# Fused attention, convolution gate and spectral mixing on one core: three moves of small work in the first stage

## The chip, the core and the metric

The kernel runs on one core of a Trainium2 chip. Five engines work side by side, each with a queue that it takes strictly in order: TensorE (PE; its weight loads are listed apart as PEld), VectorE (DVE), ScalarE (ACT), GpSimd (POOL) and SyncE (SP), which here only issues transfers. An instruction whose input is not ready holds up all that stands behind it on its engine. The metric is the device time of one execution in microseconds, and less is better.

## What is computed

Three layers follow each other, for 4 batches of 448 positions; 12 heads of 64 make 768 channels:

```python
x = softmax(causal(q @ k.T / 8)) @ v                # per batch and head
gate = sigmoid(sum(conv_w[k] * x_shifted_by(4 - k) for k in range(5)))
x = (gate * (x @ w_val)) @ w_out
theta = x @ w_theta
u = x + w_tok_r @ (x * cos(theta)) + w_tok_i @ (x * sin(theta))
out = u + maximum(u @ w_ch, 0)
```

## The kernel before

The weights arrive as raw 64-bit floats. `to_f32` makes 32-bit ones of them in three instructions (DVE L174, ACT L177, DVE L178). For the large products every operand is split into a rounded high part and the rest, a low part, and three TensorE products stand for one. `split_w` does this for half (`g` is 0 or 1) of the weight block `n`: six blocks of 128 columns for each of the four matrices, so `n` runs from 0 to 23 in the first batch. `pool_hi` (L116) writes the high part on POOL in the first batch. The low part is a subtraction, on DVE (`dve_lo`, L122) for `n` up to `AHEAD` = 2 and for some others, else on POOL (`pool_lo`, L119). The tiles are called w_ahead for blocks 0 and 1 and w_hl for the rest.

Attention goes by pairs of heads, `g` from 0 to 23, six for a batch. `attn_iter(g)` is a generator with ten steps. It transposes the probabilities of pair g-1 (`attn_PT`, L373, copied out to pt at L384 on ACT or L382 on DVE), computes the scores of pair g in two halves (`attn_S`: products L350, the row maximum L358 on DVE, the exponential L131 on ACT), turns q and k of the next pair (`attn_T`, L323 to L329), multiplies with v (L395), normalises into x (L469 on DVE, tile xf) and splits x (high part L474 on ACT). `attn_X2` then applies the five taps of the convolution, for the first six pairs on POOL (L490, L494, L497), and ends with the tanh that makes the gate (`exp_set`, L131, tile gate, on ACT).

The main program has two parts. A loop of 70 steps `n` runs the attention of the first batch alone, with the first weight blocks, and `gemm_ahead` (L518) adds each x at once into the first two output blocks of the value product. I call it the first stage; an iteration is ten of its steps. `setup_conv` at step 5 loads the 30 rows of convolution weights, turns them on TensorE (L168) and keeps them as cw. Then `dense(b)` runs the products of batch b (`gemm`, L539), with the attention of the next batch woven in by a table of rates; L577 joins gate and value, tile hf. Tile, the framework, orders the instructions of each engine by a schedule of its own that it makes when the kernel is built, so a change in one place can move neighbours. Tiles come from rings of buffers, and a new use waits until the last reader of the old one is done; xf has two buffers, so pair g+2 can be written only when POOL has read pair g.

Of the kernel before, what the change touches and what calls it, by code (L numbers as in the profile page):

```python
# [13 lines left out]
AF = mybir.ActivationFunctionType  # L14
# [14 lines left out]
Z_DVE = (0, 0, 1, 0)  # L29
AHEAD = 2  # L30
W_AT = 10
W_FROM = 2
YLD = 1
ABS_DVE = (1, 0, 0, 0)
# [13 lines left out]
def kernel(  # L48
# [36 lines left out]
    NW = 4 * KC  # L85
# [25 lines left out]
    def psum(tag):  # L111
        at = "mm" if tag == "mm" else "at"
        return ps.tile([P, 512], F32, tag=at, name=f"ps_{tag}", bufs=2 if tag == "mm" else 6)
# [10 lines left out]
    exps = []  # L124
    sins = []

    def exp_set(*args, **kw):
        with ExitStack() as st:
            if sins:
                st.enter_context(tc.issue_after(sins[-1].ins))  # L130
            exps.append(nc.scalar.activation(*args, **kw))  # L131
# [24 lines left out]
        for t in xf:  # L156
            nc.vector.memset(t[:, 0:PAD], 0.0)

    def setup_conv():
        t = pool.tile([P, CV, 2], I32, tag="wb", name="cv_raw", bufs=8)  # L160
        nc.sync.dma_start(
            out=t[: KW * KC, 0:P, :].rearrange("p n two -> p (n two)"),
            in_=conv_w.rearrange("k (c n) -> (k c) n", n=2 * P),
        )
        c32 = pool.tile([P, S], F32, tag="tmp", name="c32")[:, 0:P]
        to_f32(c32[: KW * KC, :], t[: KW * KC, 0:P, :])
        pt = psum("tr")
        nc.tensor.transpose(pt[:, : KW * KC], c32[: KW * KC, :], ident[: KW * KC, : KW * KC])  # L168
        nc.vector.tensor_copy(cw.rearrange("p k c -> p (k c)"), pt[:, : KW * KC])
# [60 lines left out]
    def split_w(n, g):  # L230
        if (n, g) not in bits:
            return
        flat = words(bits.pop((n, g))).bitcast(F32)
        t = flat.rearrange("p (c n) -> p c n", n=P)
        kept = n % NW // KC in PLAIN
        if B > 1 and kept and n < NW:
            nc.sync.dma_start(out=plain[n, g], in_=flat)
        store = B > 1 and (kept and B > 2 if n >= NW else not kept)
        if n < AHEAD:
            hi, lo = (  # L240
                pool.tile([P, S], F32R, tag=tag, name="w_ahead", bufs=12)[:, : KH * P].rearrange("p (c n) -> p c n", n=P)
                for tag in ("act_hi", "act_lo")
            )
        else:
            hl = pool.tile([P, 2, KH, P], F32R, tag="wb", name="w_hl", bufs=8)
            hi, lo = hl[:, 0], hl[:, 1]
        if n < NW:
            pool_hi(hi, t)
        else:
            nc.scalar.copy(hi, t)  # L250
        (dve_lo if n <= AHEAD or n < NW and int(W_DVE[n // KC]) > g else pool_lo)(lo, t, hi)
        if store and n < AHEAD:
            for a, x in enumerate((hi, lo)):
                nc.sync.dma_start(
                    out=scratch[n, g][:, a * KH * P : (a + 1) * KH * P], in_=f32(x.rearrange("p c n -> p (c n)"))
                )
        elif store:
            nc.sync.dma_start(out=scratch[n % NW, g], in_=f32(hl.rearrange("p a c n -> p (a c n)")))
        splits[n, g] = (hi, lo)
# [21 lines left out]
    av = {}  # L281
    x_hl = {}
    gates = {}
    rbs = {}
    row_at = {}
    wides = {}
# [191 lines left out]
    def attn_X2(g):  # L478
        b, hp = divmod(g, NP)
        x = xf[g % 2]  # L480
        gt = pool.tile([P, S], F32, tag="gate", name="gate", bufs=6)
        if CONV_ACT[g]:
            nc.scalar.activation(gt, x[:, 0:S], AF.Copy, scale=cw[:, 0, hp : hp + 1])
            for t in range(1, KW):
                tp = pool.tile([P, S], F32, tag="tmp", name="tp")
                nc.scalar.activation(tp, x[:, t : t + S], AF.Copy, scale=cw[:, t, hp : hp + 1])
                nc.gpsimd.tensor_tensor(out=gt, in0=gt, in1=tp, op=ALU.add)
        elif CONV_POOL[g]:
            tp = pool.tile([P, S], F32, tag="tmp", name="tp")
            nc.gpsimd.tensor_scalar(  # L490
                out=gt, in0=x[:, 0:S], scalar1=cw[:, 0, hp : hp + 1], scalar2=1.0, op0=ALU.mult, op1=ALU.mult
            )
            for t in range(1, KW):
                nc.gpsimd.tensor_scalar(  # L494
                    out=tp, in0=x[:, t : t + S], scalar1=cw[:, t, hp : hp + 1], scalar2=1.0, op0=ALU.mult, op1=ALU.mult
                )
                nc.gpsimd.tensor_tensor(out=gt, in0=gt, in1=tp, op=ALU.add)  # L497
        else:
            nc.vector.tensor_scalar(out=gt, in0=x[:, 0:S], scalar1=cw[:, 0, hp : hp + 1], scalar2=None, op0=ALU.mult)
            for t in range(1, KW):  # L500
                nc.vector.scalar_tensor_tensor(
                    out=gt, in0=x[:, t : t + S], scalar=cw[:, t, hp : hp + 1], in1=gt, op0=ALU.mult, op1=ALU.add
                )
        exp_set(gt, gt, AF.Tanh, scale=0.5)
        gates[b, hp] = gt

    wn = [AHEAD]
    ahead = {}
# [50 lines left out]
    def dense(b):  # L559
# [8 lines left out]
        for e in range(KC):  # L568
            if b == 0 and e < AHEAD:
                pt = ahead.pop(e)  # L570
                if YLD:
                    yield
            else:
                pt = yield from gemm(xs)
            hf = pool.tile([P, S], F32, tag="tmp", name="hf")
            hf_ins.append(
                nc.vector.scalar_tensor_tensor(  # L577
                    out=hf, in0=gates.pop((b, e)), scalar=1.0, in1=pt[:, :S], op0=ALU.add, op1=ALU.mult
                )
            )  # L580
            h_hl[e] = hl(hf, dve=H_LO[b])
            yield
# [106 lines left out]
    def attn_iter(g):  # L689
        h = g - 1  # L690
        head = g <= NP
        attn_PT(h, 0)
        attn_PT(h, 1)
        yield
        attn_S(g, 0)
        yield
        attn_PT(h, 2)
        attn_PT(h, 3)
        yield
        attn_S(g, 1)  # L700
        yield
        if head:
            attn_T(g + 1)
            load_qk(g + 3, "q")
            load_qk(g + 3, "k")
            yield
            if h in wides:
                attn_W(h)
        attn_AV(h)
        if not head:  # L710
            load_v(g + 1)
        attn_B(h)
        yield
        if not head:
            attn_T(g + 1)
            load_qk(g + 3, "q")
            load_qk(g + 3, "k")
        if head or g == B * NP:
            attn_X(h)
        if not head:  # L720
            yield
        if g < B * NP:
            attn_R(g)
        yield
        if NP < g < B * NP:
            attn_X(h)
        yield
        yield
        if head:
            load_v(g + 1)  # L730
        yield
# [16 lines left out]
    for n in range(5 * H + 10):  # L748
        next(at, None)
        if n == 5:  # L750
            setup_conv()
        if 1 <= n < 5 * H:
            with tc.issue_after(ttr_ins[-1].ins):
                for at_n, (m, g) in zip(A_TILES, ((0, 0), (1, 0), (0, 1), (1, 1), (2, 0), (2, 1), (3, 0), (3, 1))):
# [62 lines left out]
```

## Time and profile before

| | |
|---|---|
| median of 3 runs | 712.16 us (711.78 to 712.94) |
| the profiled execution | 713.53 us |
| its span in the trace | 711.7 us |
| PE busy | 676.3 us, 95% of the span |
| DVE, ACT, POOL busy | 390.4, 359.3, 304.6 us |

How to read it: the span runs from the first instruction to the last, and 1.8 us of the execution lie outside it. PE is nearly always busy over the whole, and this average hides that the first 87 us are unlike the rest. In the first stage the four compute engines pass small pieces to each other, and which of them waits is read from the row of each instruction: its start, its length, and in brackets how long its engine stood idle just before and what ended the wait.

### The profile page before, as it was taken

The page shows a single profiled execution, that of the slowest core. Times are in us where ns is not written, and L with a number is a line of the kernel's source. Part 1 is how long each engine was busy: PE and PEld are TensorE (multiplying, and loading weights), DVE is VectorE, ACT ScalarE, POOL GpSimd, SP SyncE. Part 2 cuts the span into 40 slices and gives each one's busy share as a digit, 9 for nine tenths or more (in the row PEclk, how much of TensorE's full clock was granted, in tenths as well). Part 3 has the DMA queues.
Part 4 walks back from the last instruction along what each step waited for, and adds up shares of the span by engine and source line. Part 5 has one row for each costly group of instructions (what it writes and reads, how often), then busy time and mean ns, then how long its engine had stood idle before and what let it go on. Part 6 is the DMA issues. An engine that isn't in the chain of part 4 may idle for free.

```text
span 711.7 us, 12896 instructions
## 1 busy us (share of the span) xinstructions
PE 676.3 (95%) x4595; PEld 582.3 (82%) x4595; DVE 390.4 (55%) x944; ACT 359.3 (50%) x843; POOL 304.6 (43%) x325
## 2 busy tenths in 40 slices
PE   4988798998999999999999999999999999999997
PEld 3666587776888888888888988988988899898996
DVE  4787598658766553554654545653766332126521
ACT  4657467668867445556663233345864212234401
POOL 0388967785784946751734100131611503001100
PEclk9999999999999999999999999999999999999999
DMA  7539467778661989888440668666330477672332
GB/s 210 124 96 264 121 198 218 227 227 275 181 193 49 273 274 330 257 253 250 112 129 14 172 193 238 192 181 198 116 103 14 129 213 226 214 212 74 90 102 64
DMA packets 133030, 124.67 MB, mean 175 GB/s; under 512 B 72905, under 2 KB 110567, under 8 KB 132967
## 3 DMA queue, kind: packets, MB, share of 16 engines
q1 hardware_dynamic: 132967, 123.86, 59.6%
q8 instruction: 36, 0.59, 0.3%
q14 instruction: 27, 0.22, 0.1%
HBM read 94.66 MB, written 29.16 MB: 174 GB/s over the span
## 4 chain that ended last, share of the span: by engine, by line
PE 73%; DVE 7%; POOL 6%; ACT 6%; DMA 4%; issue 2%; SPq 1%; DVEq 0%; ACTq 0%; POOLq 0%
PE ps_mm L539 42%; PE ps_mm L643 13%; PE ps_s L350 4%; PE ps_tr L373 4%; PE ps_av L395 4%; POOL gate L497 2%; PE ps_tr L629 2%; PE ps_tr L323 2%; PE ps_tr L670 1%; POOL tp L494 1%; DMA cv_raw<-in_moe_w_out_dram 1%; DVE ps_cv L174 1%; DMA cv_raw<-in_moe_w_theta_dram 1%; ACT prob L131 1%; SPq L298 1%
## 5 line engine op out<-in xcount | busy, mean ns | idle before, releaser
L539 PE MATMUL ps_mm<-act_hi,w_hl 128*128 128x448 f32 x864 | 268.8, 375 | 4.1 <-POOL w_hl L116 2.3
L539 PEld LDWEIGHTS ps_mm<-act_hi,w_hl 128*128 128x128 f32 x864 | 161.8, 189 | 23.1 <-POOL w_hl L116 3.2
L539 PE MATMUL ps_mm<-act_lo,w_hl 128*128 128x448 f32 x432 | 157.1, 364 | 0.0
L131 ACT ACTIVATE prob<-ps_s,negm 128x192 f32<-128x192 f32 (+6 forms) x168 | 79.6, 476 | 64.7 <-DVE negm L358 63.6
L358 DVE CUSTOM_DVE_ANT_0 ps_s<-ps_s,mask 128x192 f32<-128x192 f32 (+6 forms) x168 | 70.2, 437 | 69.9 <-PE ps_s L350 34.2
L539 PEld LDWEIGHTS ps_mm<-act_lo,w_hl 128*128 128x128 f32 x432 | 81.7, 189 | 4.4
L539 PE MATMUL ps_mm<-x_hi,w_hl 128*128 128x448 f32 x264 | 81.9, 376 | 0.2 <-DVE hf L577 0.2
L119 POOL TENSOR_TENSOR act_lo<-x2f,act_hi 128x448 fp32r<-128x448 f32 x36 | 41.7, 1159 | 82.2 <-ACT act_hi L553 29.6
L119 POOL TENSOR_TENSOR w_hl<-cv_raw,w_hl 128x384 fp32r<-128x384 f32 x60 | 62.9, 1050 | 18.8 <-ACT w_hl L250 17.2
L119 POOL TENSOR_TENSOR x_lo<-xf,x_hi 128x448 fp32r<-128x448 f32 x22 | 28.1, 1278 | 94.1 <-ACT x_hi L474 93.2
L643 PE MATMUL ps_mm<-wtok_h,zt_h 128*128 128x448 f32 x168 | 63.9, 381 | 0.8 <-ACT zt_h L634 0.8
L643 PE MATMUL ps_mm<-wtok_h,zt_l 128*128 128x448 f32 x168 | 62.2, 371 | 0.2
L350 PE MATMUL ps_s<-kt,qt 64*64 64x256 f32 (+6 forms) x672 | 57.4, 406 | 4.2 <-ACT pt L384 3.4
L643 PE MATMUL ps_mm<-wtok_l,zt_h 128*128 128x448 f32 x168 | 61.4, 365 | 0.0
L497 POOL TENSOR_TENSOR gate<-gate,tp 128x448 f32<-128x448 f32 x48 | 57.1, 1190 | 2.6
L373 PE MATMUL ps_tr<-ident,prob 128*128 128x128 f32 x384 | 55.0, 278 | 2.6 <-DVE cv_raw L178 2.4
L350 PEld LDWEIGHTS ps_s<-kt,qt 64*64 64x64 f32 x672 | 30.6, 137 | 29.6 <-issue 15.5
L539 PEld LDWEIGHTS ps_mm<-x_hi,w_hl 128*128 128x128 f32 x264 | 50.1, 190 | 5.1 <-DVE hf L577 0.9
L620 POOL TENSOR_TENSOR z<-z,x2f 128x448 f32<-128x448 f32 x18 | 21.5, 1197 | 74.2 <-ACT z L615 74.2
L373 PEld LDWEIGHTS ps_tr<-ident,prob 128*128 128x128 f32 x384 | 45.6, 142 | 8.9 <-DVE cv_raw L178 3.4
L395 PEld LDWEIGHTS ps_av<-pt,v 128*64 128x64 f32 x768 | 40.0, 137 | 13.6 <-ACT prob L131 3.0
L395 PE MATMUL ps_av<-pt,v 128*64 128x64 f32 (+3 forms) x768 | 48.0, 277 | 2.9 <-ACT pt L384 1.7
(103 smaller groups left out, 1126.9 us busy)
## 6 DMA issues: line engine op xcount, KB each, us to landing
w_hl<-scratch SPq DMA_DIRECT2D x120, 384.0 KB
scratch<-w_hl SPq DMA_DIRECT2D x48, 384.0 KB
q_raw<-in_q_dram SPq DMA_DIRECT2D x48, 112.0 KB
k_raw<-in_k_dram SPq DMA_DIRECT2D x48, 112.0 KB
out_dram<-o SPq DMA_DIRECT2D x24, 224.0 KB
v<-in_v_dram SPq DMA_DIRECT2D x48, 96.0 KB
cv_raw<-in_moe_w_val_dram SPq DMA_DIRECT2D x12, 384.0 KB
plain<-cv_raw SPq DMA_DIRECT2D x24, 192.0 KB
```

Of the source, the lines that this page charges most:

```text
L119: nc.gpsimd.tensor_tensor(out=dst, in0=src, in1=f32(hi), op=ALU.subtract)
L131: exps.append(nc.scalar.activation(*args, **kw))
L323: nc.tensor.transpose(pt[:, c * CP : (c + 1) * CP], t[:, c, :, :].rearrange("p h d -> p (h d)"), ident[:CP, :CP])
L350: nc.tensor.matmul(bank[o : o + D, off : off + n], lhsT=qt[j * D : (j + 1) * D, i * D : (i + 1) * D], rhs=kt[j * D : (j + 1) * D, :n], sta ...
L358: ttr = nc.vector.tensor_tensor_reduce(out=pt, in0=pt, in1=mask[:, S - n : S], scale=-1.0 / math.sqrt(D), scalar=3.0e38, op0=ALU.add, op1= ...
L373: nc.tensor.transpose(pt[:, n * P : (n + 1) * P], probs[i][:, kc * P : (kc + 1) * P], ident)
L395: mm = nc.tensor.matmul(av[g][j * D : (j + 1) * D, lo * D : hi * D], lhsT=tv[:, j, kc, :], rhs=t[:, n0 : n0 + hi - lo, o : o + D], start=( ...
L497: nc.gpsimd.tensor_tensor(out=gt, in0=gt, in1=tp, op=ALU.add)
L539: nc.tensor.matmul(pt[:, :S], lhsT=a[:, kc % KH, :], rhs=x, start=kc == 0 and m == 0, stop=kc == KC - 1 and m == 2,)
L620: (nc.vector if Z_DVE[b] else nc.gpsimd).tensor_tensor(out=t, in0=t, in1=x2f[e], op=ALU.mult)
L629: nc.tensor.transpose(pt[:, (m - m0) * P : (m - m0 + 1) * P], z.rearrange("p a s -> p (a s)")[:, m * P : (m + 1) * P], ident,)
L643: nc.tensor.matmul(pt[:, :S], lhsT=a[:, m, :], rhs=w[:, m, :], start=m == 0 and n == 0, stop=m == NZ - 1 and n == 2,)
```

## The change

Three edits. First, for blocks 0 to 2 the high part is a copy on ACT (the existing `nc.scalar.copy`, L250) instead of `pool_hi` on POOL; that is six instructions of 128x384. Second, the tanh of a gate is no longer part of `attn_X2`. The raw gate is put in a list, and `turn_gate` does the tanh in the next iteration but behind the first half of its scores, and not before two raw gates are waiting; a gate still raw when `dense` wants it is turned there. This holds for all batches. Third, the convolution weights are loaded at step 5 as before and turned at step 12, in the second iteration.

```diff
+CONV_AT = 12
...
-    def setup_conv():
+    def load_conv():
         t = pool.tile([P, CV, 2], I32, tag="wb", name="cv_raw", bufs=8)
         nc.sync.dma_start(
...
+        return t
+
+    def setup_conv(t):
         c32 = pool.tile([P, S], F32, tag="tmp", name="c32")[:, 0:P]
...
-        if n < NW:
+        if AHEAD < n < NW:
             pool_hi(hi, t)
         else:
             nc.scalar.copy(hi, t)
...
+    raw_gates = []
...
-        exp_set(gt, gt, AF.Tanh, scale=0.5)
         gates[b, hp] = gt
+        raw_gates.append((b, hp))
+
+    def turn_gate(key):
+        raw_gates.remove(key)
+        gt = gates[key]
+        with tc.issue_after(exps[-1].ins):
+            exp_set(gt, gt, AF.Tanh, scale=0.5)
...
+            if (b, e) in raw_gates:
+                turn_gate((b, e))
             hf = pool.tile([P, S], F32, tag="tmp", name="hf")
...
         attn_S(g, 0)
+        if len(raw_gates) > 1:
+            turn_gate(raw_gates[0])
         yield
...
         if n == 5:
-            setup_conv()
+            conv_raw = load_conv()
+        if n == CONV_AT:
+            setup_conv(conv_raw)
```

What stands in the queues now is shown at three places. The first is TensorE at the start of the second iteration, before the change; ident is the unit matrix of a transpose, c_215 the convolution weights, prob the probabilities of pair 0.

```order
L323 MATMUL ps_tr<-ident,k_raw 128x112 x4
L168 MATMUL ps_tr<-ident,c_215 128x30
L373 MATMUL ps_tr<-ident,prob_77 128x128 x4
L373 MATMUL ps_tr<-ident,prob_72 128x128
L373 MATMUL ps_tr<-ident,prob_75 128x128 x3
L350 MATMUL ps_s<-kt,qt 64x448 x2
```

The same place of TensorE after the change, down to the second half of the scores.

```order
L328 MATMUL ps_tr<-ident,k_raw 128x112 x4
L378 MATMUL ps_tr<-ident,prob_77 128x128 x4
L378 MATMUL ps_tr<-ident,prob_72 128x128
L378 MATMUL ps_tr<-ident,prob_75 128x128 x3
L355 MATMUL ps_s<-kt,qt 64x448 x2
L355 MATMUL ps_s<-kt,qt 64x320 x2
L355 MATMUL ps_s<-kt,qt 64x128 x2
L378 MATMUL ps_tr<-ident,prob_76 128x128 x3
L378 MATMUL ps_tr<-ident,prob_71 128x128
...
L172 MATMUL ps_tr<-ident,c_271 128x30
L355 MATMUL ps_s<-kt,qt 64x384 x2
```

The transpose of the convolution weights has moved from the head of the iteration to behind both groups of probability transposes.

The second place is ACT in the last two iterations of the first stage, before the change; xf_85 is x of pair 5, and act_hi belongs to the dense part.

```order
L474 CAST x_hi<-xf_84 128x448
L131 ACTIVATE gate<-gate 128x448
L384 COPY pt<-ps_tr 128x4x128
L384 COPY pt<-ps_tr 128x2x2x128
L131 ACTIVATE prob_77,sums<-ps_s,negm 128x448
...
L443 COPY rb<-ps_tr 128x448
L131 ACTIVATE prob_74,sums<-ps_s,negm 128x256
L131 ACTIVATE gate<-gate 128x448
L474 CAST x_hi<-xf_85 128x448
L555 CAST act_hi<-hf 128x448 x2
```

The same stretch of ACT after the change.

```order
L479 CAST x_hi<-xf_84 128x448
L389 COPY pt<-ps_tr 128x4x128
L389 COPY pt<-ps_tr 128x2x2x128
L132 ACTIVATE prob_77,sums<-ps_s,negm 128x448
...
L132 ACTIVATE prob_72,sums<-ps_s,negm 128x128
L132 ACTIVATE gate<-gate 128x448
L132 ACTIVATE prob_76,sums<-ps_s,negm 128x384
...
L132 ACTIVATE prob_74,sums<-ps_s,negm 128x256
L479 CAST x_hi<-xf_85 128x448
L566 CAST act_hi<-hf 128x448 x2
```

The tanh has left the place ahead of the copies of pt and of x_hi, and stands between two exponentials.

The third place is POOL over the convolutions of pairs 0 and 1, before the change.

```order
L497 TENSOR_TENSOR gate<-gate,tp 128x448
L494 TENSOR_SCALAR tp<-xf_84,cw 128x448
L116 TENSOR_SCALAR w_ahead<-cv_raw 128x384
L497 TENSOR_TENSOR gate<-gate,tp 128x448
L494 TENSOR_SCALAR tp<-xf_84,cw 128x448
L497 TENSOR_TENSOR gate<-gate,tp 128x448
L116 TENSOR_SCALAR w_ahead<-cv_raw 128x384
L490 TENSOR_SCALAR gate<-xf_85,cw 128x448
```

The same place of POOL after the change.

```order
L502 TENSOR_TENSOR gate<-gate,tp 128x448
L499 TENSOR_SCALAR tp<-xf_84,cw 128x448
L502 TENSOR_TENSOR gate<-gate,tp 128x448
L499 TENSOR_SCALAR tp<-xf_84,cw 128x448
L502 TENSOR_TENSOR gate<-gate,tp 128x448
L495 TENSOR_SCALAR gate<-xf_85,cw 128x448
```

The high parts of the weights have gone from between the taps.

## Rows read from the trace of the kernel before

**Rows 1.** Busy time by stretch: start:end, length, engines' busy us, clock, DMA share.

```profile
12.00:87.00 75.00, 59.66 (x575) 44.99 (x573) 52.36 (x156) 48.02 (x143) 52.72 (x62) 1.00 0.65 167
97.00:115.00 18.00, 18.00 (x133) 14.86 (x132) 18.00 (x44) 12.91 (x32) 9.31 (x12) 1.00 0.82 249
183.00:705.00 522.00, 519.16 (x3399) 458.11 (x3398) 257.81 (x587) 237.16 (x537) 180.47 (x177) 1.00 0.57 168
```

**Rows 2.** PE timeline, second iteration: start, length, instruction, [idle before <- releaser].

```profile
15.88 0.28 PE L168 MATMUL ps_tr<-ident,c 30*128 30x30 f32 x1 [3.69 <-DVE c L178]
...
18.00 1.77 PE L350 MATMUL ps_s<-kt,qt 64*64 64x448 f32 x12
```

**Rows 3.** Timeline of DVE over the same stretch.

```profile
14.80 0.28 DVE L174 TENSOR_SCALAR ps_cv<-cv_raw 30x128 int32<-30x128 uint32 x1 [1.48 <-DMA cv_raw<-in_moe_conv_w_dram]
...
15.67 0.60 DVE L329 COPY kt<-ps_tr 128x448 f32<-128x448 f32 x1
16.20 0.54 DVE L174 TENSOR_SCALAR ps_cv<-cv_raw 128x384 int32<-128x384 uint32 x1
...
19.80 0.63 DVE L358 CUSTOM_DVE_ANT_0 ps_s<-ps_s,mask 128x448 f32<-128x448 f32 x1 [0.26 <-PE ps_s L350]
```

**Rows 4.** Timeline of DVE, the six writes of x in the first stage.

```profile
28.93 0.61 DVE L469 TENSOR_TENSOR xf<-ps_av,rb 128x448 f32<-128x448 f32 x1
...
40.93 0.62 DVE L469 TENSOR_TENSOR xf<-ps_av,rb 128x448 f32<-128x448 f32 x1
...
51.45 0.61 DVE L469 TENSOR_TENSOR xf<-ps_av,rb 128x448 f32<-128x448 f32 x1
...
63.94 0.62 DVE L469 TENSOR_TENSOR xf<-ps_av,rb 128x448 f32<-128x448 f32 x1
...
73.78 0.61 DVE L469 TENSOR_TENSOR xf<-ps_av,rb 128x448 f32<-128x448 f32 x1
...
84.10 0.59 DVE L469 TENSOR_TENSOR xf<-ps_av,rb 128x448 f32<-128x448 f32 x1
```

**Rows 5.** Timeline of DVE, three low parts of weights.

```profile
36.33 1.50 DVE L122 TENSOR_TENSOR w_ahead<-cv_raw,w_ahead 128x384 fp32r<-128x384 f32 x1 [1.04 <-POOL w_ahead L116]
...
41.65 0.58 DVE L122 TENSOR_TENSOR w_ahead<-cv_raw,w_ahead 128x384 fp32r<-128x384 f32 x1
...
55.42 1.48 DVE L122 TENSOR_TENSOR w_hl<-cv_raw,w_hl 128x384 fp32r<-128x384 f32 x1 [1.56 <-POOL w_hl L116]
```

**Rows 6.** Timeline of POOL: one tap, and what follows the sixth convolution.

```profile
36.26 1.16 POOL L497 TENSOR_TENSOR gate<-gate,tp 128x448 f32<-128x448 f32 x1
...
95.96 0.52 POOL L116 TENSOR_SCALAR w_hl<-cv_raw 128x384 fp32r<-128x384 f32 x1 [0.67 <-issue]
96.56 1.02 POOL L119 TENSOR_TENSOR w_hl<-cv_raw,w_hl 128x384 fp32r<-128x384 f32 x1
```

**Rows 7.** Timeline of ACT, where it waits in the first stage.

```profile
38.26 0.47 ACT L131 ACTIVATE prob<-ps_s,negm 128x256 f32<-128x256 f32 x1 [2.32 <-DVE negm L358]
...
57.47 0.53 ACT L131 ACTIVATE prob<-ps_s,negm 128x320 f32<-128x320 f32 x1 [2.28 <-DVE negm L358]
...
76.58 0.58 ACT L131 ACTIVATE gate<-gate 128x448 f32<-128x448 f32 x1 [1.60 <-POOL gate L497]
77.07 1.05 ACT L384 COPY pt<-ps_tr 128x512 f32<-128x512 f32 x2
...
85.90 0.58 ACT L131 ACTIVATE gate<-gate 128x448 f32<-128x448 f32 x1 [2.46 <-POOL gate L497]
86.38 0.55 ACT L474 CAST x_hi<-xf 128x448 fp32r<-128x448 f32 x1
```

**Rows 8.** Timeline of PE at the end of the first stage and at the fifth value block.

```profile
86.98 0.67 PE L518 MATMUL ps_mm<-x_hi,w_ahead 128*128 128x448 f32 x2 [2.39 <-ACT x_hi L474]
...
99.53 0.47 PE L539 MATMUL ps_mm<-x_hi,w_hl 128*128 128x448 f32 x1
```

**Rows 9.** Groups of instructions: ACT's copies of later weights; busy us, mean ns.

```profile
L250 ACT CAST w_hl<-cv_raw 128x384 fp32r<-128x384 f32 x24 | 12.3, 511 | 13.0 <-POOL w_hl L119 5.0 <-issue 3.3 <-DMA cv_raw<-plain 3.0
```

## The prediction, made before the result was known

> **What bounds the kernel now.** I read the busy times by stretch first. From 183 to 705 us PE is busy 519.16 of 522 us [rows 1]: nothing can be won there, and whatever is gained earlier arrives at the end as long as PE is not made to wait anew. Between 12 and 87 us PE is busy only 59.66 of 75 us; the 15.3 us it stands idle are the ceiling for this change, since its own work stays as it is. POOL is busy 52.72 us there, nearly all of it behind the first x at 29 us, so it has hardly a pause from then on.
>
> Then I followed the timelines to see what each engine waits for. The six writes of x [rows 4] give the pace: 12.00, 10.52, 12.49, 9.84 and 10.32 us between them. The 9.84 shows what an iteration costs when little goes wrong. Three patterns go wrong. (1) PE idles 3.69 us in front of the transpose of the convolution weights [rows 2], because DVE waited 1.48 us for their transfer [rows 3]; the softmax of pair 0 stood ready behind it. (2) Low parts on DVE wait for high parts that stand in POOL's queue behind taps: 1.04 us at 36.33 and 1.56 us at 55.42, and then run 1.50 and 1.48 us where the free one at 41.65 takes 0.58 [rows 5]. ACT's next exponential then waits 2.32 and 2.28 us [rows 7]. (3) The tanh waits on ACT for POOL's last tap, 1.60 us at 76.58 with the copies of pt behind it, 2.46 us at 85.90 with x_hi behind it [rows 7], for which PE waits 2.39 us [rows 8].
>
> **The change, part by part.**
>
> Convolution weights. Their load is issued as before; what moves is one DVE pair, one ACT piece, one 0.28 us transpose and a copy of cw. PE can start the transposes of the probabilities at about 12.2 (15.88 less 3.69) and be through at 14.2. The scores then need kt, which was at 15.67 behind the 1.48 us wait. The order now puts one piece of a weight block (0.54 us for its like at the same place) ahead of kt, so kt is about 0.8 us earlier, done at 15.5, and the scores start at 15.5 instead of 18.00 [rows 2, 3]. The first maximum stood 1.80 us behind that start (19.80 less 18.00), which gives 17.3; the small pieces of the convolution weights now run on DVE just ahead of it, so I take 17.8, a gain of 2.0. The write of x then also stands ahead of a low part (0.58) instead of behind it: 2.5 together. Bounds: 1.0 (the 1.48 wait less the 0.54 piece) and 3.7 (the whole idle time). cw is needed for the first tap behind x. In the new order its copy stands a few pieces behind the first maximum (17.8), so near 20, some 6 us ahead of x, and its later turn is covered; were it not, the taps of pair 0 would be late by as much, and nobody asks for that gate for another iteration.
>
> High parts on ACT. Six leave POOL, four of them between taps, and ACT takes over six of 0.51 us [rows 9]. The lows no longer wait for POOL's queue. At 36.33 the wait and the excess are 1.04 + 0.92 = 1.96; at 55.42 they are 2.46, of which ACT's wait behind it lets 2.28 through. That is 4.2 gained. But the excess needs a second look. The tap that started at 36.26 ran until 37.42 [rows 6] and the low part until 37.83, while the one at 41.65 with no such addition beside it took 0.58: a low part that meets a POOL addition costs 0.92 more. Before, two of four met one; I take two again, 1.8, so 2.4 remain. Bounds: 4.2 (none meets one) and 0.5 (all four do, 3.7). In the third iteration the order now has a copy and a low part ahead of x, where x stood first: 0.8 lost, bounds 0 and 1.1 (0.51 + 0.58). The other copies lie in ACT's pauses, of which 12 to 87 us has 27 (75 less 48.02, [rows 1]).
>
> On the excess the Trainium skill has a rule (SBUF — State Buffer, section "Who interferes with whom"): a DVE instruction with two SBUF inputs and a GpSimd instruction that reads SBUF take the same port in turn, and the one that started first holds it to its end. The row at 36.33, which ends 0.41 us behind the tap's end, agrees. By this rule the change does nothing about the excess, since only the waits for POOL's queue go.
>
> The tanh. The five of the first stage that stood in the open leave their places. At 76.58 the 1.60 wait and 0.49 of work (77.07 less 76.58) go from in front of pt: 2.1. At 85.90 x_hi could start when x is done, 84.7, instead of 86.38: 1.7. Together 3.8; bounds 2.5 and 3.8, since pt may find a new wait. At the new place, behind the exponential of 128 columns in the next iteration, the gate has been ready for some microseconds, so there is no wait, but four of them cost up to 0.49 each between exponentials: I take 1.5, bounds 0 and 2.0, nearer the upper end because DVE and ACT hand pieces to and fro there. The tanhs of pairs 4 and 5 now stand in the dense part behind softmax work, and the two gate products (hf) that want them come a little later: 0.4 lost, bounds 0 and 1. What is queued behind hf on DVE is raw-weight work for blocks some 5 us off. In the later batches the tanh moves within ACT's slack while PE is full: 0, and 0.5 either way from the altered order.
>
> Sum: -2.5 - 2.4 + 0.8 - 3.8 + 1.5 + 0.4 = -6.0 us. Against the profiled execution, 713.53 - 6.0 = 707.5; that one lies 1.4 us above the median of the runs, so against 712.16 it is 706.2.
>
> **What is late next.** Behind the first stage DVE is busy 18.00 of 18 us from 97 to 115 [rows 1], a packed chain that starts with the first gate product, so it should move as a whole. POOL's next duty is the split of value block 4: its low part is done at 97.6 (96.56 + 1.02) and PE wants it at 99.53 [rows 6, 8], a slack of 1.9. POOL comes free of the sixth convolution at 95.3 (95.96 less 0.67). It starts 2.5 earlier and drops four high parts, 2.0; with the slack, 6.5 us can be gained before PE waits for POOL even if POOL keeps every pause, and more if its pauses close too.
>
> **The rivals.**
>
> A, the lows collide. All four of the lows meet a tap's addition, as the rule of the page named above would allow at any time. For it: POOL's taps fill most of an iteration. Against: two of four missed them before. Price 1.8 more than I took: gain 4.2, 708.0.
>
> B, everything hides. No low meets an addition, tanh and copies lie in pauses: 2.5 + 4.2 + 3.8 less the 0.4 is 10.1, and POOL's pauses must then close for it; I take 9.5, 702.7. For it: 15.3 us of idle PE. Against: the hand-overs on DVE and ACT are tight.
>
> C, given back. The dense part's weight transfers do not come earlier, PE waits for them between 115 and 183 us, and the time is 712 as before. For it: DMA is at 0.82 of its time from 97 to 115 [rows 1]. Against: at 0.65 before that it has room, and a load is issued when the products free a buffer, which then happens earlier.
>
> D, slower. ACT becomes what PE waits for. It decides if the copies, which wait for DVE, hold up pt and the exponentials in each iteration: six times 0.51 plus a wait of the same size is 6.1, four lows at 0.92 are 3.7, four tanhs 2.0, together 11.8, against the lowest gains, 1.0 + 2.5 and the two bare waits 2.6: 5.7 slower, 717.9. Against it: ACT is busy 48.02 of 75 us [rows 1].
>
> That the change does not do what it says I leave without a chance: the order shows all three moves.
>
> **How the numbers follow.** Forecast 0.56, A 0.17, B 0.13, C 0.10, D 0.04. The forecast's own range is 704.5 to 708. To hold 8 in 10 it must reach from B to beyond A, so 702.6 to 709.5. A measurement of this kernel can tell about 0.2%, 1.4 us, from no change. The forecast, A and B are faster: 0.86. C is mostly within 0.2%: 0.09 with its near misses; slower is D and a part of C, 0.05.
>
> **What would show it.** The first x at about 26.4 instead of 28.93; the paces of the second and fourth iteration near 10.5 instead of 12.00 and 12.49, the third longer than 10.52; no wait of ACT in front of a tanh; x_hi of pair 5 right behind its x, and the gap of 2.39 us on PE at 86.98 below 1; the first product after it (86.98) at about 80.5. PE from 183 us on should look as before, only earlier. The prediction is wrong if pt's copies still come 2 us behind x, if a new wait on the copied high parts stands on DVE or ACT, or if PE's idle time between 97 and 183 us grows by what was won.

## The result, and the profile after

| | before | after |
|---|---|---|
| median | 712.55 us (711.78 to 713.98) | 702.31 us (701.54 to 705.05) |
| the profiled execution | 713.53 us | 702.1 us |
| its span in the trace | 711.7 us | 700.2 us |
| PE busy | 676.3 us, 95% | 673.8 us, 96% |

The ratio is 0.9863, with a 95% interval of 0.9843 to 0.9884: 9.8 us gained (8.3 to 11.2), where 6.0 were forecast. The median lies 3.9 us below the forecast and 0.3 us below the low end of the range. The sign was right; the size was not.

The changed kernel's busy times by stretch, columns as in [rows 1] (start:end, length, busy us of PE, PEld, DVE, ACT and POOL, clock, DMA share, GB/s):

```profile
12.00:87.00 75.00, 66.23 (x611) 51.10 (x610) 58.73 (x171) 52.71 (x156) 56.17 (x62) 0.98 0.67 170
97.00:115.00 18.00, 17.04 (x126) 14.22 (x128) 15.24 (x39) 14.78 (x35) 13.62 (x16) 1.00 0.88 251
183.00:694.00 511.00, 509.04 (x3339) 450.36 (x3338) 249.61 (x570) 228.12 (x521) 175.31 (x171) 1.00 0.57 169
```

Against [rows 1], PE stands idle 8.8 us between 12 and 87 us instead of 15.3. The packed stretch of DVE (18.00 of 18 us from 97 to 115) now begins earlier, so that 97 to 115 shows its end.

The timeline of DVE in the changed kernel (start, length, instruction, [idle before <- releaser]), for [rows 3 to 5]; L474 is the write of x, L123 a low part, L590 the gate product:

```profile
14.27 0.61 DVE L334 COPY kt<-ps_tr 128x448 f32<-128x448 f32 x1
...
17.01 0.61 DVE L363 CUSTOM_DVE_ANT_0 ps_s<-ps_s,mask 128x448 f32<-128x448 f32 x1
...
24.55 0.62 DVE L474 TENSOR_TENSOR xf<-ps_av,rb 128x448 f32<-128x448 f32 x1
...
31.18 0.55 DVE L123 TENSOR_TENSOR w_ahead<-cv_raw,w_ahead 128x384 fp32r<-128x384 f32 x1
...
34.99 0.61 DVE L474 TENSOR_TENSOR xf<-ps_av,rb 128x448 f32<-128x448 f32 x1
...
46.17 0.62 DVE L474 TENSOR_TENSOR xf<-ps_av,rb 128x448 f32<-128x448 f32 x1
...
47.84 0.71 DVE L123 TENSOR_TENSOR w_hl<-cv_raw,w_hl 128x384 fp32r<-128x384 f32 x1 [0.58 <-ACT w_hl L254]
...
57.38 0.61 DVE L474 TENSOR_TENSOR xf<-ps_av,rb 128x448 f32<-128x448 f32 x1
...
68.17 0.61 DVE L474 TENSOR_TENSOR xf<-ps_av,rb 128x448 f32<-128x448 f32 x1
...
76.28 0.59 DVE L474 TENSOR_TENSOR xf<-ps_av,rb 128x448 f32<-128x448 f32 x1
...
97.89 0.60 DVE L590 SCALAR_TENSOR_TENSOR hf<-gate,ps_mm 128x448 f32<-128x448 f32 x1
```

The first x comes at 24.55 instead of 28.93. The paces are 10.44, 11.18, 11.21, 10.79 and 8.11 us, where [rows 4] give 12.00, 10.52, 12.49, 9.84 and 10.32. The low parts that took 1.50 and 1.48 us [rows 5] take 0.55 and 0.71.

The timeline of ACT in the changed kernel, the first three rows for [rows 7], the others for two places in the later batches:

```profile
58.03 0.56 ACT L479 CAST x_hi<-xf 128x448 fp32r<-128x448 f32 x1 [2.74 <-DVE xf L474]
...
68.81 0.57 ACT L479 CAST x_hi<-xf 128x448 fp32r<-128x448 f32 x1 [3.11 <-DVE xf L474]
...
76.90 0.56 ACT L479 CAST x_hi<-xf 128x448 fp32r<-128x448 f32 x1 [1.00 <-DVE xf L474]
...
153.69 0.56 ACT L132 ACTIVATE gate<-gate 128x448 f32<-128x448 f32 x1
154.16 0.53 ACT L607 ACTIVATE z<-ps_mm 128x448 int32<-128x448 f32 x1
154.58 0.58 ACT L389 COPY pt<-ps_tr 128x512 f32<-128x512 f32 x1
...
370.46 1.28 ACT L132 ACT_TABLE_LOAD   x1
...
374.09 0.56 ACT L132 ACTIVATE gate<-gate 128x448 f32<-128x448 f32 x1
```

No tanh waits any more, and ACT waits for x itself. The timeline of PE in the changed kernel, its larger waits up to 160 us, for [rows 2] and [rows 8]:

```profile
15.03 1.77 PE L355 MATMUL ps_s<-kt,qt 64*64 64x448 f32 x12 [2.63 <-DVE rec L417]
...
77.52 0.68 PE L529 MATMUL ps_mm<-x_hi,w_ahead 128*128 128x448 f32 x2 [0.74 <-ACT x_hi L479]
...
107.94 0.47 PE L550 MATMUL ps_mm<-act_lo,w_hl 128*128 128x448 f32 x1 [0.87 <-DVE act_lo L123]
...
155.22 1.12 PE L400 MATMUL ps_av<-pt,v 128*64 128x256 f32 x4 [2.35 <-ACT pt L389]
```

The 3.69 us in front of the convolution's transpose have become 2.63 in front of the scores, and the 2.39 us in front of the last products of the first stage 0.74. The wait for pt at 155 us was 1.71 before, at 165.44, so it grew.

**Where the gain lies.** The table gives the length of each piece in the trace of every kernel run: from the first scores to the first x, the five iterations up to the sixth x, on to the third and to the sixth gate product of the first batch, to the first gate product of the second batch, to that of the third, and to the end.

| kernel | first scores at | to x 1 | to x 6 | to gate 3 | to gate 6 | to batch 2 | to batch 3 | to the end |
|---|---|---|---|---|---|---|---|---|
| before | 7.19 | 21.74 | 55.17 | 11.62 | 17.55 | 152.45 | 164.19 | 281.79 |
| after | 6.71 | 17.84 | 51.73 | 10.09 | 18.03 | 151.50 | 162.91 | 281.39 |
| e10, changed again | 7.31 | 17.86 | 51.71 | 10.09 | 18.03 | 151.84 | 162.91 | 281.35 |
| e1, convolution alone | 7.10 | 18.39 | 55.56 | 11.62 | 17.88 | 153.70 | 164.16 | 281.79 |
| e2, high parts alone | 7.18 | 21.56 | 53.48 | 11.40 | 17.54 | 151.10 | 164.27 | 281.27 |
| e3, tanh alone | 7.04 | 21.93 | 54.29 | 10.10 | 18.02 | 150.34 | 162.91 | 281.87 |
| e4, all but tanh | 7.07 | 17.86 | 53.07 | 11.61 | 17.55 | 151.18 | 164.10 | 281.36 |
| e5, all but convolution | 7.23 | 21.02 | 51.47 | 10.10 | 18.02 | 150.51 | 162.90 | 281.45 |
| e6, all but high parts | 7.19 | 18.38 | 54.66 | 10.11 | 18.04 | 150.79 | 162.97 | 281.66 |
| e7, tanh late in batch 1 only | 6.72 | 17.85 | 51.72 | 10.09 | 18.01 | 150.39 | 164.18 | 281.44 |
| e8, pieces later | 7.23 | 18.55 | 51.82 | 10.10 | 18.03 | 149.75 | 163.18 | 281.14 |
| e9, block 3 on ACT | 7.14 | 17.85 | 51.35 | 10.10 | 18.05 | 149.63 | 162.91 | 281.37 |
| e12, the same again | 7.25 | 17.85 | 51.37 | 10.11 | 18.01 | 150.03 | 163.42 | 281.26 |
| e11, block 3, early in batch 2 | 7.26 | 17.85 | 51.38 | 10.10 | 18.02 | 149.10 | 162.93 | 281.46 |

The second row has its first scores 0.48 us earlier, from a transfer that landed earlier; e10 shows that this is no part of the change. Against before it gains 3.88, 3.46 and 1.53 us in the first stage, loses 0.48, and gains 0.61, 1.28 and 0.44 behind it.

### The profile page after: what moved, and what is told of

Its sections match the earlier page's. It is cut to its first block, busy times and chain, and to the rows that moved or that the text cites. A ratio compares the mean times of both kernels' runs of the same rounds, so it can differ in the third digit from the quotient of the medians.

```text
span 700.2 us, 12875 instructions
## 1 busy us (share of the span) xinstructions
PE 673.8 (96%) x4595; PEld 581.7 (83%) x4595; DVE 386.9 (55%) x944; ACT 358.7 (51%) x849; POOL 302.9 (43%) x319
## 4 chain that ended last, share of the span: by engine, by line
PE 74%; ACT 8%; DVE 7%; DMA 5%; POOL 4%; issue 2%; SPq 0%; DVEq 0%; POOLq 0%; ACTq 0%
PE ps_mm L550 42%; PE ps_mm L656 14%; PE ps_av L400 5%; PE ps_s L355 4%; PE ps_tr L378 4%; DMA cv_raw<-in_moe_w_out_dram 2%; ACT prob L132 2%; PE ps_tr L642 2%; PE ps_tr L328 2%; PE ps_tr L683 1%; POOL gate L502 1%; DMA cv_raw<-in_moe_w_theta_dram 1%; DVE ps_cv L178 1%; DVE ps_s L363 1%; DVE cv_raw L182 1%
## 5 line engine op out<-in xcount | busy, mean ns | idle before, releaser
L400 PE MATMUL ps_av<-pt,v 128*64 128x128 f32 (+3 forms) x768 | 49.6, 281 | 3.3 <-ACT pt L389 2.4
```

The costliest lines, as they stand in the source:

```text
L400: mm = nc.tensor.matmul(av[g][j * D : (j + 1) * D, lo * D : hi * D], lhsT=tv[:, j, kc, :], rhs=t[:, n0 : n0 + hi - lo, o : o + D], start=( ...
```

## The experiments

Three theories. S: each edit removes its own waits and the gains add up. P: the convolutions on POOL are the chain of the first stage, so only what shortens POOL's queue, or starts it earlier, counts. K: the gain beyond the forecast is PE's clock, which stood at 0.57 between 88 and 92 us of the trace before, behind the 2.39 us gap.

### One edit alone, and all but one: e1 to e6

The first three are the kernel before with one of the three edits of the diff above. The other three are the changed kernel with one edit undone:

```diff
 e4, the tanh at once:
+        exp_set(gt, gt, AF.Tanh, scale=0.5)
         gates[b, hp] = gt
-        raw_gates.append((b, hp))
 e5, the convolution weights at step 5:
-CONV_AT = 12
+CONV_AT = 5
 e6, the high parts on POOL:
-        if AHEAD < n < NW:
+        if n < NW:
             pool_hi(hi, t)
```

> The kernel before with the convolution weights turned at step 12 and nothing else. Theory S (the three edits are worth something each, and add up): the trace after has the first x 4.38 us earlier, of which 0.5 lies at the very start (kt of pair 0 at 5.93 instead of 6.42, a transfer that landed earlier); so 3.9 us, median near 708.6 where the kernel before has 712.5. Theory P (the convolutions on POOL are the chain of the first stage): the same 3.9, as all taps stand behind the first x. Theory K (the extra gain is PE's clock, which stood at 0.57 in 88 to 92 us of the trace before behind a gap of 2.39 us): the edit alone gains the 2.5 of the prediction, 710.0, and the low clock behind the last convolution stays.

> The kernel before with the high parts of blocks 0 to 2 on ACT and nothing else. Theory S: two waits of DVE behind POOL go (1.04 and 1.56 us) and no low part meets a POOL addition, as in the trace after: 4.2 less the 0.8 in the third iteration, 3.4, median near 709.1. Theory P: it takes four high parts of 0.5 us from POOL's chain as well, 4.5 to 5.5, so 707 to 708. Theory K: 2.4 less 0.8 as predicted, 1.6, 710.9.

> The kernel before with the tanh of a gate moved an iteration later and nothing else. Theory S: the two open waits of ACT go, 3.8 less 1.9 for the new places, 2 to 3 us, median near 709.5 to 710.5. Theory P: the tanh was never in POOL's chain, so only the tail behind the sixth x can gain: 1.7, 710.8. Theory K: the gap of 2.39 us on PE falls below 1 and the clock does not drop behind it; that saves 1.75 us of clock on top, 4 to 5.5 in all, 707 to 708.5.

> The changed kernel with the tanh back at the end of the convolution. Theory S: 702.5 plus 2 to 3, so 704.5 to 705.5. Theory P: 702.5 plus 1.7, 704.2. Theory K: the gap in front of the last products of the first stage is back at over 2 us, with a low clock behind it: 706.5 to 708.

> The changed kernel with the convolution weights turned at step 5 again. Theory S: 702.5 plus 3.9, near 706.4. Theory P: the same 3.9. Theory K: 702.5 plus 2.5, 705.0.

> The changed kernel with the high parts of blocks 0 to 2 on POOL again. Theory S: 702.5 plus 3.4, near 705.9. Theory P: 702.5 plus 4.5 to 5.5, 707 to 708. Theory K: 702.5 plus 1.6, 704.1.

| | median | ratio to before, 95% interval | in us of 712.5 |
|---|---|---|---|
| e1, convolution alone | 711.16 | 0.9959 (0.9939 to 0.9978) | -2.9 |
| e2, high parts alone | 709.53 | 0.9948 (0.9928 to 0.9967) | -3.7 |
| e3, tanh alone | 709.26 | 0.9941 (0.9921 to 0.9960) | -4.2 |
| e4, all but tanh | 706.92 | 0.9904 (0.9885 to 0.9923) | -6.8 |
| e5, all but convolution | 704.55 | 0.9885 (0.9866 to 0.9904) | -8.2 |
| e6, all but high parts | 705.49 | 0.9901 (0.9884 to 0.9918) | -7.1 |

Each edit alone is worth something, and its worth beside others is the difference of two rows (or of a row and all three): the convolution 1.6 to 3.1 us, the high parts 2.7 to 4.0, the tanh 2.9 to 4.5. Such a difference is known to some 2 us, so the 1.6 is not told apart from nothing; the others are. The three alone add up to 10.8 where all together give 9.8. That is S in its form, though the tanh was worth more than the 2 to 3 us written down and the convolution less than 3.9. P falls with the tanh, for which it had 1.7 (and 4.5 to 5.5 for the high parts). K's numbers fit the tanh (4 to 5.5) and, better than S's, the convolution (2.5), but not the high parts (1.6). Its mechanism does not carry the gain: in e10 7.3 of the 10.6 us lie ahead of the sixth x, and from 12 to 87 us the clock of before stood at 1.00 [rows 1] and that of after at 0.98. The busy times of the stretch behind the last gap, of before and then of e2, columns as above:

```profile
80.00:100.00 20.00, 17.35 (x110) 13.96 (x109) 15.34 (x36) 11.05 (x27) 17.17 (x19) 0.91 0.40 105
```

```profile
80.00:100.00 20.00, 18.36 (x125) 15.34 (x124) 15.97 (x33) 11.00 (x26) 15.34 (x17) 1.00 0.52 144
```

In e2 the gap is 1.25 us and the clock stays at full speed (2.4 GHz); before, it fell to half for some 3.5 us. Yet from the first to the third gate product both take 7.30 us (86.32 to 93.62, and 88.43 to 95.72, 7.29). PE does fewer products in that time (32 before, 39 in e2), so the low clock puts work off, but the third gate product does not wait for it.

What the work put off costs further on is not settled. The trace after has a clock of 0.98 between 97 and 183 us and e10 has 1.00, with 151.50 and 151.84 us up to the second batch, which shows no price. But e1, whose low stretch lasts from 83.6 to 90.3 us, twice as long as before, takes 1.6 us more than before from the third gate product to the second batch. And over 114 runs on record a mean clock that is lower by 0.001 goes with a time that is longer by 0.15 us within one kernel, where the lost clock by itself would be 0.7. The mean clock was 0.989 before and is 0.994 with the change. I estimate 0.8 us of the gain from that slope; at the full price it would be 3.6, nearly the whole excess over the forecast, but the places of the gain speak against it.

### The tanh by batches: e7

```diff
         gates[b, hp] = gt
+        if b > 0:
+            exp_set(gt, gt, AF.Tanh, scale=0.5)
+            return
         raw_gates.append((b, hp))
```

> The changed kernel, but from the second batch on the tanh stands at the end of the convolution again; only the first batch keeps it an iteration later. Theory S (each place adds its own): all three kernels that keep the early tanh show a wait of 0.76 to 0.79 us on PE near 381 us, behind a table load and a tanh on ACT, and about 1.25 us are lost there; the others don't have it. So this kernel loses 1.25 us against the changed one, 1.0 to 1.5 in the span, and the rest of the tanh's gain stays: near 703.6. The prediction had 0 here, 0.5 either way: 702.0 to 702.8.

702.87 us, ratio 0.9869 (0.9852 to 0.9887): no difference from the changed kernel that can be told. S's 703.6 did not come. But two things lie under it. From the second batch to the third it takes 164.18 us, as all kernels with early tanhs do (164.10 to 164.27), and late ones 162.90 to 163.42. And it reaches the second batch in 150.39 us instead of 151.50. The timeline of PE in e7, the wait for pt and the wait in the third batch's attention:

```profile
154.41 1.52 PE L400 MATMUL ps_av<-pt,v 128*64 128x256 f32 x18 [1.71 <-ACT pt L389]
...
370.23 0.47 PE L659 MATMUL ps_mm<-wtok_h,zt_h 128*128 128x448 f32 x1 [0.76 <-ACT zt_h L650]
```

The kernel before has the same wait at 381 us. Its timeline of ACT there shows why:

```profile
378.18 1.28 ACT L131 ACT_TABLE_LOAD   x1
380.07 0.58 ACT L131 ACTIVATE gate<-gate 128x448 f32<-128x448 f32 x1 [0.61 <-POOL gate L497]
380.55 1.82 ACT L634 CAST zt_h<-ps_tr 128x512 fp32r<-128x512 f32 x4
```

A table load and a tanh that waits for POOL stand ahead of the four copies that PE wants. With the late tanh the copies go first (the load is at 370.46 and the tanh at 374.09 in the rows of after). In the second batch it is the other way round: the late tanh at 153.69 and one more piece stand right ahead of the copy of pt for which PE waits 2.35 us; early, that wait is 1.71. So the later batches' move gains 1.27 in one place and loses 1.1 on the way to the second batch, of which this wait is 0.64 (0.46 against e10, where it is 2.17). The gain in the third batch is there in all kernels, 0.7 to 1.4 us between any late one and any early one. The loss is not: e3, late as well, needs only 150.34 us for that piece, and e4, with the early tanh, has a wait of 2.48 us for the same pt, behind a piece of a weight block that waited for DVE. So the cause of the 1.1 stays open, and the place of the tanh explains at most the 0.64.

### Pieces still later: e8

```diff
-CONV_AT = 12
+CONV_AT = 14
-A_TILES = (10, 14, 22, 28, 34, 40, 46, 52)
+A_TILES = (12, 14, 22, 28, 34, 40, 46, 52)
```

> The changed kernel with more of the small work taken from in front of the second iteration: the first weight piece is turned at step 12 instead of 10, the convolution weights at 14 instead of 12. Theory S: PE's remaining wait of 2.63 us in front of the scores of pair 1 is DVE's queue; without the weight piece (0.60 us) ahead of kt and the low part (0.54) ahead of the first maximum, x of pair 0 comes 0.6 to 1.1 earlier than 24.55 and the time is 701.4 to 701.9. Rival: the moved pieces come back later in the same iteration, ahead of x, and nothing is left: 702.5, the first x within 0.3 of 24.55.

701.18 us, ratio 0.9854 (0.9830 to 0.9878): not told apart from the changed kernel. The first x is at 25.78, from equal starts 0.7 us later than there (18.55 against 17.84 in the table). The rival had the mechanism, though it expected the first x within 0.3 us: what S moves away comes back in the same iteration, and with interest. Behind the first stage e8 makes this good (149.75 us to the second batch for 151.50), for which neither had a reason. The timeline of PE in e8:

```profile
15.05 1.77 PE L355 MATMUL ps_s<-kt,qt 64*64 64x448 f32 x12 [2.34 <-ACT prob L132]
...
21.73 0.24 PE L172 MATMUL ps_tr<-ident,c 30*128 30x30 f32 x1 [1.41 <-DVE c L182]
```

The scores do start 0.5 us earlier, counted from the first scores (15.05 less 7.23, against 15.03 less 6.71), and now wait for an exponential of ACT's instead of DVE. But the transpose of the convolution weights is something again that PE waits for, 1.41 us, ahead of the second iteration's product with v.

### Block 3 too: e9, e12, e11, beside e10

```diff
 e9 and e12:
-        if AHEAD < n < NW:
+        if AHEAD + 1 < n < NW:
             pool_hi(hi, t)
 e11, besides:
         gates[b, hp] = gt
+        if b == 1:
+            exp_set(gt, gt, AF.Tanh, scale=0.5)
+            return
         raw_gates.append((b, hp))
```

> The changed kernel with the high parts of block 3 on ACT too, two more copies. Theory S: the hand-overs on DVE, not POOL's load, were what the second edit repaired; the low parts of block 3 are on POOL, so no wait of DVE goes, and ACT gets 2 x 0.5 us more: 702.5 to 703.5. Theory P (POOL is the chain): 1.0 us less on POOL, 701.5.

> The changed kernel once more, as it is, for the comparison with the two below on one chip. Every theory expects 702 to 703. The profile tells what repeats of its waits: 2.63 us in front of the scores of pair 1 and 2.35 us in front of the product with v at 155 us should be there again. The granted clock of 0.96 behind the latter may be there or not; if it is not, the span is 1 to 1.7 us shorter with the same waits.

> The changed kernel with the high parts of block 3 on ACT, once more beside the changed kernel. If these two copies are worth something by themselves, it is again 1.5 to 2 us below the changed kernel. If its 700.45 came from the stretch behind the first stage, where its trace had no low clock, it is within 0.7 us of it: the two traces agree until 104 us (last gate product of the first batch at 104.49 and 104.40 with a start 0.43 later).

> The changed kernel with the high parts of block 3 on ACT, and with the tanh at the end of the convolution in the second batch alone. Theory S: the run with early tanhs from the second batch on got from the first stage to the second batch in 150.4 us instead of 151.5, since the tanh no longer stands ahead of pt at 153.7, and lost 1.27 us in the third batch; early in the second alone it keeps the 1.1 and does not pay the 1.27. With block 3 as in the run before: 699 to 700. Rival: the 1.1 is what varies from run to run (a stretch of low clock); then as the kernel below, within 0.5 us.

| | median | ratio to before, 95% interval |
|---|---|---|
| e9, block 3 on ACT | 700.45 | 0.9834 (0.9817 to 0.9850) |
| e10, changed again | 703.04 | 0.9857 (0.9831 to 0.9882) |
| e12, block 3 on ACT again | 701.19 | 0.9831 (0.9805 to 0.9857) |
| e11, block 3, early in batch 2 | 701.51 | 0.9835 (0.9811 to 0.9860) |

Two more copies on ACT gave a lower median both times, the second time 1.9 us below the changed kernel on the same chip (runs of 700.31 to 702.32 against 702.13 to 703.90); the intervals of the two ratios still touch. S had said 702.5 to 703.5, and that was wrong. P had the number (701.5) but not the place: in the first stage the two copies save 0.34 us (51.71 to 51.37), no more. The rest arises behind it. At 105 us e12 is 0.41 ahead of e10, behind the wait for pt 0.8, from 241 us to the second batch 2.2, and 1.7 to 1.8 from the third batch to the end. The timeline of PE at 241 us, in e10 and then in e12:

```profile
239.50 0.98 PE L355 MATMUL ps_s<-kt,qt 64*64 64x384 f32 x8
240.91 0.97 PE L355 MATMUL ps_s<-kt,qt 64*64 64x192 f32 x8 [0.44 <-ACT prob L132]
```

```profile
238.44 1.22 PE L355 MATMUL ps_s<-kt,qt 64*64 64x384 f32 x16
```

In e10 the scores come in two pieces with a wait for an exponential between them and take 2.4 us (239.50 to 241.88); in e12 the same products run through in 1.22. Why the hand-over is met in one and missed in the other stays open: it was not tried, and the orders differ in many places by then. e11 confirms that the tanh can be early in the second batch and late in the third (149.10 and 162.93 us), but its median is not told apart from e12's: the 699 to 700 of S did not come, and the rival's number did.

e10 repeats both waits of the changed kernel, as 2.84 us in front of the scores and 2.17 in front of the product with v, without the low clock behind the second. Its span is 0.9 us longer, 0.6 of it in the first transfers, and not 1 to 1.7 shorter, as was expected without that low clock.

## Why the prediction was right and wrong

**The convolution weights, -2.5.** The mechanism was right: in e1, where nothing else is changed, the scores start at 15.42 (15.5 forecast). That the first maximum then stands at 17.82 (17.8) is luck in part. The timeline of DVE in e1:

```profile
17.15 0.56 DVE L123 TENSOR_TENSOR w_ahead<-cv_raw,w_ahead 128x384 fp32r<-128x384 f32 x1 [0.41 <-POOL w_ahead L117]
...
17.82 0.61 DVE L363 CUSTOM_DVE_ANT_0 ps_s<-ps_s,mask 128x448 f32<-128x448 f32 x1
...
25.49 0.62 DVE L474 TENSOR_TENSOR xf<-ps_av,rb 128x448 f32<-128x448 f32 x1
```

A low part stands ahead of the maximum and waits 0.41 us for a high part on POOL. It is the first of the waits that the second edit takes away (0.72 us at 18.98 in the kernel before), and the prediction counted only the later two. In e4, with the high parts on ACT too, it is gone, and the maximum comes 1.99 us behind the start of the scores (15.39) instead of 2.40. The timeline of DVE in e4:

```profile
16.64 0.54 DVE L123 TENSOR_TENSOR w_ahead<-cv_raw,w_ahead 128x384 fp32r<-128x384 f32 x1
...
17.38 0.61 DVE L363 CUSTOM_DVE_ANT_0 ps_s<-ps_s,mask 128x448 f32<-128x448 f32 x1
```

What was mis-sized is the way from the maximum to x, which took 9.13 us before and for which I only took off a low part. It took 7.67: the waits of DVE for ACT's exponentials on it went from 2.35 us (0.91, 0.80, 0.64) to 1.18; why they shrank is not shown. With the start taken out e1 gains 3.35 here, and beside other edits this one is worth 3.2 to 3.7 on the way to the first x (e5 and after, e2 and e4, e3 and e6 in the table), up to the upper bound of 3.7. The 3.88 of the changed kernel hold some 0.5 of the high parts as well (18.39 in e1, 17.86 in e4). At the end 2.9 arrive alone, and 1.6 as the last of the three edits: the way to the second batch is 1.0 to 1.3 us longer with it (151.50 and 151.84) than without (150.51 in e5).

**The high parts, -2.4 + 0.8.** The two waits for POOL went as said. Of the second 0.58 us came back, for the copy on ACT (the low part at 47.84), which is in small what the prediction named as a sign of being wrong. The step that failed is "two of four met one; I take two again". None did in the changed kernel. In the eight traces up to e6 with the two kernels compared, 40 low parts stand between 20 and 60 us. Ten took 1.30 to 1.50 us, and each of these began while a POOL operation with two inputs (an addition or a subtraction) was running; the other thirty took 0.54 to 0.71, with a POOL multiplication running, or nothing, or an operation that began behind them. With the high parts on POOL there are exactly two long ones in each kernel, always those that POOL's high part released onto an addition or, once each in e3 and e6, a subtraction: the high part ends, POOL takes its next instruction, and DVE starts 0.07 us behind it (36.26 and 36.33 in [rows 5, 6]). Where that next one is a multiplication, the low part takes 0.58. So the collision was no chance of two in four. The wait made it. With the copy on ACT a long one hangs on the order: e2 and e4, with the early tanh, have one each; the eight traces with the late tanh in the first batch (the changed kernel twice, e5, e7, e8, e9, e11 and e12) have none. The timeline of DVE and then of POOL in e2, the low part and the subtraction that it met:

```profile
51.75 1.31 DVE L123 TENSOR_TENSOR w_hl<-cv_raw,w_hl 128x384 fp32r<-128x384 f32 x1 [0.58 <-ACT w_hl L254]
```

```profile
51.51 1.13 POOL L120 TENSOR_TENSOR x_lo<-xf,x_hi 128x448 fp32r<-128x448 f32 x1
```

And POOL in the changed kernel, beside the low part at 31.18 and at the place of the one above, where the low part at 47.84 came first:

```profile
31.14 1.01 POOL L499 TENSOR_SCALAR tp<-xf,cw 128x448 f32<-128x448 f32 x1
...
47.50 0.64 POOL L499 TENSOR_SCALAR tp<-xf,cw 128x448 f32<-128x448 f32 x1
48.10 1.43 POOL L120 TENSOR_TENSOR x_lo<-xf,x_hi 128x448 fp32r<-128x448 f32 x1
```

There POOL's subtraction pays, 1.43 instead of 1.13. The Trainium skill (SBUF — State Buffer, section "Who interferes with whom") says that the order of issue decides who blocks; the rows with two inputs on both engines agree. Those with a multiplication on POOL do not: the low part at 47.84 began 0.34 us into one and took 0.71 us instead of 0.55, well short of waiting for its end, and the one at 31.18 began 0.04 us behind one and took 0.55, while the multiplication took 1.01 instead of 0.64. The sentence of the prediction that by this rule the change does nothing about the excess drew the wrong conclusion, since the change moves the order of issue.

By iterations: the second gains 1.9 (12.38 to 10.47, e1 to e4), as said. The fourth gains 0.5, where the row promised more, since other waits are next there (pt, 0.91 us before the scores at 59.62 in the changed kernel). The 0.8 lost in the third is not to be seen (10.53 to 10.45). The sum of the five iterations is -1.69 alone and -2.5 to -2.9 beside other edits, for a forecast of -1.6.

**The tanh, -3.8 + 1.5 + 0.4.** All three terms held. The sixth x comes 2.2 us sooner behind the fifth (10.32 to 8.12, e3), 2.1 forecast; from there to the third gate product it takes 10.10 instead of 11.62, 1.5 for 1.7. At the new places the third and fifth iterations lose 1.1 and 0.95 and the fourth wins 0.8 back: 1.3 for 1.5. The gate products of pairs 4 and 5 lose 0.48 for 0.4; the row at 97.89 stands 8.4 us behind the gate product ahead of it (89.52), where before it was 5.4, and the next one makes most of that good. PE's next wait is 0.87 us for act_lo at 107.94; before it was 2.30 for POOL, at 118.88.

**"In the later batches ... 0, and 0.5 either way."** This failed. It is -0.61 to the second batch, -1.28 to the third and -0.44 behind it in e10. The 1.28 is the tanh's, shown by e7. The stretch up to the second batch does not move as a whole, as the part on what is late next had it: it takes 149.1 to 153.7 us in kernels that differ only ahead of it or by a few pieces. It was not worked out from any row which way that would go, so 0.5 was too narrow a bound.

**The account.** Against 6.0 forecast the trace of e10 gives 10.6: 1.4 more up to the first x (some 0.5 of it the high parts'), 1.3 more in the iterations (3.46 for 1.6 and 0.6), 2.3 more behind the first stage, less 0.3 up to the sixth gate product and 0.1 of start. That is the difference, 4.6.

**The rivals.** A (collisions) and D (ACT as the bound) did not come; ACT is busy 52.71 of 75 us. C did not either: the wait for pt grew by 0.5 to 0.6, but the stretch around it is 0.6 to 1.0 shorter as a whole. B's 702.7 is the number that came, and half of its mechanism: no low part met an addition, but the tanh kept its price of 1.3, and what B lacked came from the way to the first x and from the third batch; that its number came is luck in part. POOL's cap of 6.5 us was no cap, since its pauses closed: it is busy 56.17 us from 12 to 87, with six high parts fewer, instead of 52.72, and PE waits for no split of POOL's up to 97 us. The range ended at B's 702.7 less 0.1; with the later batches' 2 us in it, it would have held.

**The marks.** The first x was due at 26.4 and came at 24.55 (25.17 in e10, which starts as late as before); the second and fourth iteration at 10.5 and came at 10.44 and 11.21; the third longer than 10.52, 11.18. No tanh waits, the gap at the end of the first stage is 0.74, and the product behind it begins at 77.52 for 80.5. PE's idle time between 97 and 183 us did not grow (6.6 us before, 6.1 after).

## What to carry to other kernels

An instruction that waits for another engine starts at the same moment as that engine's next one: if the two share something, the wait brings a collision with it, as in all eight long low parts that a high part on POOL released here. When a piece is moved out of one place, look up who stands behind it at each of its new places in every stage, also those in which the engine seems to have slack: the later batches' two places came to 1.27 and -1.1 us in e7, the second without a full explanation. And a stretch of packed work behind the change is not a rigid block; kernels that differ by a few pieces ahead of it took 149.1 to 153.7 us for it here, so such a spread belongs in the range.

## What the runs showed of the hardware that I had not expected

In the first 190 us of the traces PE's clock fell to half (1.2 GHz) around or behind waits of 1.5 to 4.6 us, for some 3.5 us and in e1 and e2 once for some 6.7, but not behind all of them: the kernel before has a wait of 3.69 us at 15.88, and e3 one of 2.92 at 161.63, with the clock at full speed behind it. Two pairs of traces with and without a low stretch show no price for it, at the end of the first stage (7.29 and 7.30 us) and behind it (151.50 and 151.84). Over the 114 runs there is one, a fifth of what the lost clock would be by itself (0.15 us of 0.7).

The first stage is steadier than the medians: of the changed kernel's two traces the pieces up to the sixth gate product agree within 0.02 us, and the scatter is in the first transfers (6.71 against 7.31) and in the stretch up to the second batch (151.50 against 151.84). The two traces of e9 and e12, one kernel as well, part in that stretch (149.63 and 150.03) and in the next (162.91 and 163.42).
